# Weight sums made by pairs of tiles on VectorE, token sums moved from GpSimd to VectorE, and another order at the ends of blocks, in a fused attention and two-layer FFN kernel

## The chip, the cores and the metric

One core of a Trainium2 chip. The metric is the device time in microseconds (us) of the whole program; lower is better.

## The reference, cut to what matters

Three stages in a row on B = 2, H = 8, S = 768, D = 64, so 1536 tokens of 512 features; both FFN layers have 2048 hidden features. The attention inputs are float32, the four weight matrices float64, the output float32.

```python
def reference(q, k, v, lam, moe_w_in, moe_w_out, moe2_w_in, moe2_w_out):
    x = decay_attention(q, k, v, lam)             # blockwise, with a decayed state per head
    x = x.transpose(0, 2, 1, 3).reshape(1536, 512)
    h = x @ moe_w_in                              # 512 -> 2048
    x = (h * tanh(softplus(h))) @ moe_w_out       # 2048 -> 512
    h = x @ moe2_w_in
    return (h * clip(h + 3, 0, 6) / 6) @ moe2_w_out
```

## The kernel before, in words

Every operand of the FFN products is split into a high and a low part (`split`: ScalarE copies the rounded high part, L84, and VectorE subtracts it, L87); a product takes three passes (high-high, high-low, low-high). The weights come as float64 words of 8 bytes: `to_single` (L268) makes float32 of them with two instructions on ScalarE (L272, L273) and two on VectorE (L274, L277).

The 1536 tokens are three blocks of 512. The hidden features of a layer are 16 tiles of 128: 8 "lower" and 8 "upper". A **step** n of the main loop (L507) is one block and one tile of the first layer: 12 matmuls of the first product (`gemm1`, L301) into one of two PSUM banks h, then 12 of the second product of step n - 2 (`gemm2`, L310) into four banks y; ScalarE makes the activation (`act_first`, L330 and L331), VectorE its low part (`g_lo`). There are 48 steps: blocks 0 and 1 with the lower tiles (0 to 15), block 2 with all tiles (16 to 31), blocks 0 and 1 with the upper tiles (32 to 47). Attention runs in steps 0 to 15. The last tile of a block evacuates y (`evacuate`, emitted two steps later): block 2 by four splits into X, blocks 0 and 1 by four additions to `part` (L345) and splits owed one per step (`split_owed`). The next step's `gemm2` needs these four banks again.

The first layer's weights come as planned units (`advance`, `conv_at`), the upper ones in units of 512 KB through a pool of three staging tiles. In the second half of the main loop `make_later` (L457) prepares the second layer's weights, 32 units of 512 KB from step 22 on: each is loaded into the same pool, converted, split into `low`, the memory of the lower tiles that are no longer needed, and spilled to DRAM by pairs (`spill`, L409). The second product of the second layer is done in a Strassen-like scheme with 7 products instead of 8, so a pair of tiles needs three more weight blocks, which `sub` (L443) makes with four subtractions on GpSimd (POOL), and each token operand four more sums (`combine`, L615, L620, on GpSimd).

The last stretch (L667) is 24 **runs** j, one per block and pair of tiles, 8 runs to a block. A run has two first products (12 matmuls each, L587, into one single bank h, tag "h0", that `gate`, L609 on ScalarE and L610 on VectorE, must have read before the next), each followed by a part of the second products of the run before (`second_product`, L602): 18 matmuls, then 24, into seven accumulators. Weights are fetched back from DRAM (`fetch`, L412) into slots, in an order worked out before. When a block's 8 runs are through, `close_first` and `close_second` scale the accumulators (L640), add them up (L643 to L664, two sums on GpSimd) and store four quarters (L632).

All DMAs here are issued from SyncE's queue (SP), in order. The order of instructions on each engine is set by the compiler's list scheduler, which starts from the program's order and lets instructions whose inputs it takes to be ready go ahead; `tc.keep_in_program_order(ins)` ties an instruction behind the one traced before it on its engine.

## Time and profile before

| | us |
|---|---|
| median of 3 runs (602.42 to 605.28) | 604.87 |
| the profiled execution | 600.34 |
| its span, first to last instruction | 598.6 |
| busy in it: TensorE matmul / weight load | 570.5 / 481.9 |
| VectorE / ScalarE / GpSimd | 325.1 / 274.5 / 140.0 |

The profiled execution is one more run of the same program, 4.5 us below the median. Times in rows count from the start of the span. A line of the timeline is a start, a duration and a merged group of like instructions of one engine; "[1.66 <-ACT g L331]" is the idle time of the engine before the group and what ended it. Consecutive groups of one engine overlap a little, since an instruction's latency reaches over the next one's start. PE is TensorE, DVE is VectorE, ACT ScalarE, POOL GpSimd.

### The profile page before, as it was taken

How to read it: one execution, taken by the hardware profiler on the slowest of the kernel's cores; microseconds unless marked ns; L12 is line 12 of the kernel's file. 1: busy time of each engine (PE TensorE's matmuls, PEld its weight loads, DVE VectorE, ACT ScalarE, POOL GpSimd, SP SyncE). 2: the span in 40 equal slices, each digit the busy share in tenths (PEclk: the TensorE clock that was granted, in tenths of full speed). 3: DMA queues.
4: the chain of work that ended last, by engine and by line, in shares of the span. 5: the costliest groups of instructions: out<-in, count | busy, mean ns of one | idle time of the engine just before them, and what ended most of it. 6: DMA issues, size and time to landing. Idle time of an engine off the chain costs nothing. (4 is left out here: it accounts for less than half of the span.)

```text
span 598.6 us, 8726 instructions
## 1 busy us (share of the span) xinstructions
PE 570.5 (95%) x3470; PEld 481.9 (81%) x3470; DVE 325.1 (54%) x467; ACT 274.5 (46%) x460; POOL 140.0 (23%) x154
## 2 busy tenths in 40 slices
PE   7999999999999989599999999999899999899993
PEld 3777778878888878488788889999899999799993
DVE  3799996436765575966781633334533344433433
ACT  2378775216765565755761423233332334223332
POOL 1600100000212211222020233232532323523223
PEclk9999999999999999799999999999999999999998
DMA  7979663304356688566974468400486301576202
GB/s 226 396 242 337 212 204 109 106 2 155 127 202 273 205 321 305 200 253 244 334 289 204 193 230 306 167 1 19 139 303 261 124 1 66 185 279 205 112 1 70
DMA packets 23427, 113.82 MB, mean 190 GB/s; under 512 B 2378, under 2 KB 6490, under 8 KB 17754
## 3 DMA queue, kind: packets, MB, share of 16 engines
q1 hardware_dynamic: 23386, 113.27, 52.2%
q8 instruction: 27, 0.44, 0.3%
q14 instruction: 14, 0.11, 0.1%
HBM read 87.03 MB, written 26.22 MB: 189 GB/s over the span
## 5 line engine op out<-in xcount | busy, mean ns | idle before, releaser
L620 POOL TENSOR_TENSOR F<-F 128x256 f32<-128x256 f32 x96 | 80.1, 834 | 194.1 <-DVE F L610 190.3
L310 PE MATMUL y<-g,up 128*128 128x512 f32 x288 | 71.2, 396 | 6.2 <-DVE X L87 5.9
L610 DVE SCALAR_TENSOR_TENSOR F<-x,h 128x512 f32<-128x512 f32 x48 | 32.8, 684 | 75.4 <-ACT x L609 75.4
L587 PE MATMUL h<-X,up 128*128 128x512 f32 x288 | 70.2, 392 | 2.2 <-DVE F L610 2.2
L301 PE MATMUL h<-X,low 128*128 128x512 f32 x288 | 72.0, 397 | 0.2 <-DVE state L248 0.2
L301 PE MATMUL h<-X,up 128*128 128x512 f32 x288 | 69.5, 390 | 2.4 <-ACT g L331 2.4
L443 POOL TENSOR_TENSOR st<-st 128x256 f32<-128x256 f32 x32 | 33.8, 1066 | 162.6 <-DVE st L277 148.8
L587 PE MATMUL h<-X,low 128*128 128x512 f32 x288 | 69.9, 391 | 1.6 <-DVE F L610 1.6
L310 PEld LDWEIGHTS y<-g,up 128*128 128x128 f32 x288 | 54.8, 191 | 18.8 <-DVE X L87 6.3
L310 PE MATMUL y<-g,low 128*128 128x512 f32 x288 | 69.5, 390 | 0.1
L609 ACT ACTIVATE x<-h 128x512 f32<-128x512 f32 x48 | 28.7, 597 | 81.9 <-PE h L587 81.9
L301 PEld LDWEIGHTS h<-X,up 128*128 128x128 f32 x288 | 53.9, 188 | 14.5 <-ACT g L331 3.3
L310 PEld LDWEIGHTS y<-g,low 128*128 128x128 f32 x288 | 54.0, 188 | 11.7 <-DVE low L87 0.5
L301 PEld LDWEIGHTS h<-X,low 128*128 128x128 f32 x288 | 52.8, 188 | 13.1 <-issue 1.7
L587 PEld LDWEIGHTS h<-X,up 128*128 128x128 f32 x288 | 52.5, 188 | 12.7 <-DVE F L610 2.6
L274 DVE SCALAR_TENSOR_TENSOR st<-st 128x512 int32<-128x512 int32 (+1 forms) x57 | 43.6, 768 | 34.8 <-ACT st L273 34.6
L587 PEld LDWEIGHTS h<-X,low 128*128 128x128 f32 x288 | 52.7, 188 | 11.9 <-DVE F L610 1.8
L84 ACT ACTIVATE low<-st 128x512 fp32r<-128x512 f32 (+2 forms) x57 | 39.8, 698 | 47.5 <-DVE st L277 30.4
L272 ACT ACTIVATE st<-st 128x512 f32<-128x512 f32 (+1 forms) x57 | 42.1, 739 | 35.9 <-DMA st<-w 35.6
L87 DVE TENSOR_TENSOR low<-st,low 128x512 fp32r<-128x512 f32 (+2 forms) x57 | 47.9, 845 | 18.5 <-ACT low L84 17.6
L87 DVE TENSOR_TENSOR up<-F,up 128x256 fp32r<-128x256 f32 (+2 forms) x36 | 30.4, 844 | 44.7 <-ACT up L84 44.7
L87 DVE TENSOR_TENSOR low<-F,low 128x256 fp32r<-128x256 f32 (+2 forms) x36 | 30.1, 838 | 38.8 <-ACT low L84 38.8
(59 smaller groups left out, 716.1 us busy)
## 6 DMA issues: line engine op xcount, KB each, us to landing
st<-w SPq DMA_DIRECT2D x50, 512.0 KB, 5.6
wc<-low SPq DMA_DIRECT2D x8, 1792.0 KB, 6.8
up<-wc SPq DMA_DIRECT2D x8, 1792.0 KB, 7.3
raw<-att SPq DMA_DIRECT2D x24, 512.0 KB, 5.7
low<-wc SPq DMA_DIRECT2D x6, 1792.0 KB, 7.0
wc<-low SPq DMA_DIRECT2D x8, 1024.0 KB, 6.2
up<-wc SPq DMA_DIRECT2D x8, 1024.0 KB, 4.9
st<-w SPq DMA_DIRECT2D x7, 1024.0 KB, 7.3
```

The source lines that it names most:

```text
L84: nc.scalar.activation(out=hi, in_=src, func=ACTF.Copy)
L87: nc.vector.tensor_tensor(out=lo, in0=src, in1=f32(hi), op=ALU.subtract)
L272: nc.scalar.activation(out=hf, in_=hf, func=ACTF.Copy, scale=2.0 ** -112)
L274: nc.vector.scalar_tensor_tensor(out=lo, in0=hi, scalar=-2 ** 31, in1=lo, op0=ALU.bitwise_and, op1=ALU.bitwise_or)
L301: nc.tensor.matmul(h, lhsT=W[t][:, a, kt * 128:kt * 128 + 128], rhs=X[k][:, b, kt, :], start=(kt, a, b) == order[0], stop=(kt, a, b) == or ...
L310: nc.tensor.matmul(y[e], lhsT=l, rhs=r, start=(first and i == 0), stop=(last and i == 2),)
L443: nc.gpsimd.tensor_tensor(out=o, in0=a, in1=b, op=ALU.subtract)
L587: nc.tensor.matmul(h, lhsT=w[:, a, kt * 128:kt * 128 + 128], rhs=X[k][:, b, kt, :], start=(kt, a, b) == order[0], stop=(kt, a, b) == order ...
L609: nc.scalar.activation(out=x, in_=h, func=ACTF.Relu, bias=3.0)
L610: nc.vector.scalar_tensor_tensor(out=F[:, 2 * i:2 * i + 2].rearrange("p i n -> p (i n)"), in0=x, scalar=6.0, in1=h, op0=ALU.min, op1=ALU.mult,
L620: nc.gpsimd.tensor_tensor(out=F[:, o], in0=F[:, a], in1=F[:, b], op=op)
```

## The change

The pool of three staging tiles becomes one tile `ring` with three places. `low` loses its first two tiles to a tile `low0`, whose memory becomes, at step 20, a tile `spare` (half for sums, half for staging) and later the token operand's buffer `GBUF[0]`. The second layer's weights come as 16 units u of 1 MB, a pair of tiles and one half (0: for the first product, 1: for the second) each. A unit passes two phases. `assemble(u)` converts both tiles at once into a contiguous tile and, for half 1, makes the four subtractions on VectorE; its two ScalarE instructions are kept in program order, and it issues the load of unit u + 2. `deliver(u)` splits all of it in one go (1024 or 1792 columns) and spills it. The 32 phases (A0, A1, D0, A2, D1, A3, D2, ...) are given to the steps 21 to 46, one each and two in steps 24, 27, 31, 35, 39 and 43. The first layer's last ten units are asked for in steps 16 to 20, two each.

In the last stretch the seven products get other operands (F[1] to F[7] in place), the four token sums go to VectorE (one after the first gate, three after the second) and the splits become one of 3 and one of 4 quarters; in the last run they are cut finer. The order of the products at i = 0 and 1 is (1, 4, 2) and (6, 7, 5, 3), after the last run (1, 7, 6, 5) and (4, 2, 3). The closing sums of a block (`close`) follow each product, stand behind the gate and the sums in the program, and use VectorE and ScalarE alone.

```diff
-    unit_p = ctx.enter_context(tc.tile_pool(name="unit", bufs=3, side="right"))
+    ring = tm1_p.tile([128, 3, 512], U64, tag="ring", name="ring")
...
-    low = main.tile([128, 2048 * HALF], F32R, name="low")
+    low = main.tile([128, 2048 * (HALF - 2)], F32R, name="low")
+    low0 = main.tile([128, 4096], F32R, tag="low0", name="low0")
...
-        place(t, low[:, t * 2048:(t + 1) * 2048])
+        whole, i = (low0, t) if t < 2 else (low, t - 2)
+        place(t, whole[:, i * 2048:(i + 1) * 2048])
...
-        pool = unit_p if count == 1 else stage_p
-        st = pool.tile([128, count, 512], U64, tag=f"st{count}", name="st")
+        if w is w1 and count == 2:
+            st = stage_p.tile([128, 2, 512], U64, tag="st2", name="st")
+        elif w is w1:
+            i = unit_turn[0] % 3
+            unit_turn[0] += 1
+            slots[w is w1, t, half] = {i}
+            st = ring[:, i:i + 1]
+        elif half == 0:
+            slots[w is w1, t, half] = {0, 1}
+            st = ring[:, 0:2]
+        else:
+            slots[w is w1, t, half] = {3}
+            st = spare[0][:, 8:16].bitcast(U64).rearrange("p a n -> p (a n)").rearrange("p (t n) -> p t n", t=2)
...
+
+    def to_single(st, dest=None):
...
-        nc.scalar.activation(out=hf, in_=hf, func=ACTF.Copy, scale=2.0 ** -112)
-        nc.scalar.activation(out=lo, in_=lo16, func=ACTF.Copy, scale=2.0 ** -13, bias=2.0 ** -14 - 0.5)
+        for o, i, scale, bias in ((hf, hf, 2.0 ** -112, 0.0), (lo, lo16, 2.0 ** -13, 2.0 ** -14 - 0.5)):
+            ins = nc.scalar.activation(out=o, in_=i, func=ACTF.Copy, scale=scale, bias=bias)
+            if dest is not None:
+                tc.keep_in_program_order(ins)
...
         nc.vector.scalar_tensor_tensor(
-            out=hi, in0=hi, scalar=3, in1=lo, op0=ALU.logical_shift_left, op1=ALU.bitwise_or
+            out=hi if dest is None else dest.bitcast(I32), in0=hi, scalar=3, in1=lo,
+            op0=ALU.logical_shift_left, op1=ALU.bitwise_or
...
-    later = [(2 * p + i, half) for p in range(NPAIR) for half in (1, 0) for i in range(2)]
+    later = [(p, half) for p in range(NPAIR) for half in (0, 1)]
...
     def prefetch(upto):
         while fetched[0] < min(upto, len(later)):
-            t, half = later[fetched[0]]
-            load_w(w2, t, half, 1)
+            p, half = later[fetched[0]]
+            load_w(w2, 2 * p, half, 2)
             fetched[0] += 1
...
+    def assemble(u):
+        p, half = later[u]
+        B = spare[0] if half else ring[:, 2].bitcast(F32).rearrange("p (a n) -> p a n", n=256)
+        whole = B[:, 0:4].rearrange("p (t i) n -> p t (i n)", t=2)
+        to_single(staged(w2, 2 * p, half), whole)
+        prefetch(u + 3)
         if half == 0:
-            c = w1c(p % 2)[:, i]
-            split(c[:, 0], c[:, 1], hf)
-            if i == 1:
-                spill(p, 0)
...
+            ready[u] = whole
...
+            for o, x, y in ((4, 0, 1), (5, 2, 4), (6, 2, 0), (7, 3, 5)):
+                nc.vector.tensor_tensor(out=B[:, o], in0=B[:, x], in1=B[:, y], op=ALU.subtract)
+            ready[u] = B[:, 1:8]
+
+    def deliver(u):
+        p, half = later[u]
+        c = w2c(p % 2) if half else w1c(p % 2).rearrange("p t a n -> p a t n")
+        split(c[:, 0], c[:, 1], ready.pop(u))
+        spill(p, half)
+
+    PHASES = [(assemble, 0)]
+    for u in range(1, 2 * NPAIR):
+        PHASES += [(assemble, u), (deliver, u - 1)]
+    PHASES.append((deliver, 2 * NPAIR - 1))
 
     def make_later(count):
-        for _ in range(min(count, len(later) - made[0])):
-            prefetch(made[0] + 3)
-            convert_later(made[0])
-            made[0] += 1
-            prefetch(made[0] + 2)
+        for _ in range(count):
+            f, u = PHASES.pop(0)
+            f(u)
 
...
     conv_at = {
-        1: 2, 2: 1, 3: 1, 4: 2, 5: 1, 8: 2, 11: 1, 13: 1, 14: 2, 16: 2, 17: 1, 18: 2, 20: 2, 21: 2, 24: 1,
+        1: 2, 2: 1, 3: 1, 4: 2, 5: 1, 8: 2, 11: 1, 13: 1, 14: 2, 16: 2, 17: 2, 18: 2, 19: 2, 20: 2,
     }
-    conv_first = {1, 16, 18, 20, 24}
+    conv_first = {1, 16, 18, 20}
+    twice = {24, 27, 31, 35, 39, 43}
...
@@ -553,11 +572,15 @@
         split_owed()
         if n not in conv_first:
             advance(conv_at.get(n, 0))
-        if n >= 22:
-            make_later(2 if n % 2 == 0 else 1)
+        if n == 20:
+            spare.append(main.tile([128, 16, 256], F32, tag="low0", name="spare"))
+            prefetch(2)
+        if n >= 21 and PHASES:
+            make_later(2 if n in twice else 1)
...
-    GBUF = [low[:, 11264:14848], up[2][:, 0:3584]]
+    assert not PHASES
+    GBUF = [main.tile([128, 4096], F32R, tag="low0", name="G0")[:, 0:3584], up[2][:, 0:3584]]
...
-    PRODUCT = ((1, 0, 0), (2, 1, 1), (4, 2, 6), (5, 3, 3), (7, 5, 4), (6, 4, 5), (3, 6, 2))
+    PRODUCT = {1: (0, 0), 2: (2, 2), 3: (6, 1), 4: (1, 6), 5: (3, 3), 6: (4, 4), 7: (5, 5)}
...
+    SUMS = {4: (0, 2, ALU.add), 5: (4, 1, ALU.subtract), 6: (1, 0, ALU.subtract), 7: (3, 5, ALU.subtract)}
+
+    def sums(F, which):
+        for o in which:
+            a, b, op = SUMS[o]
+            nc.vector.tensor_tensor(out=F[:, o], in0=F[:, a], in1=F[:, b], op=op)
+
+    def parts(j, F, lo, hi):
+        if j not in G_t:
+            G_t[j] = GBUF[j % 2].rearrange("p (a i n) -> p a i n", a=2, i=7)
+        G = G_t[j]
+        split(G[:, 0, lo - 1:hi - 1], G[:, 1, lo - 1:hi - 1], F[:, lo:hi])
+
+    def combine(j, F, i):
+        if j < len(runs) - 1:
+            if i == 0:
+                sums(F, (6,))
+            else:
+                sums(F, (4, 5, 7))
+                parts(j, F, 1, 4)
+                parts(j, F, 4, 8)
+        elif i == 0:
+            parts(j, F, 1, 2)
+            sums(F, (6,))
+            parts(j, F, 6, 7)
+        else:
+            sums(F, (4, 5))
+            parts(j, F, 4, 6)
+            sums(F, (7,))
+            parts(j, F, 2, 4)
+            parts(j, F, 7, 8)
...
+    def close(k, m):
+        if not rest:
+            rest[:] = homes()
+        p1, c11, p7, c22, c21, c12 = rest
+        seen.add(m)
+        if m == 1:
+            scaled(p1, 1)
+        elif m == 7:
+            scaled(p7, 7)
+        elif m == 2:
+            added(c11, 2, p1)
+            store(k, 0, 0, c11)
+        elif m == 4:
+            if 6 in seen:
+                added(c21, 4, p7)
+                store(k, 1, 0, c21)
+            else:
+                scaled(c21, 4)
+        elif m == 6:
+            added(c12, 6, p1)
+        elif m == 5:
+            added(c22, 5, p7)
+            store(k, 1, 1, c22)
+            added(c12, 5, c12)
+        elif m == 3:
+            added(c12, 3, c12)
+            store(k, 0, 1, c12)
+        if m in (6, 7) and {6, 7} <= seen:
+            plus(p7, p7, c12)
+            if 4 in seen:
+                plus(c21, c21, p7)
+                store(k, 1, 0, c21)
+        if len(seen) == 7:
+            seen.clear()
+            rest.clear()
+
...
+            which = (1, 4, 2) if i == 0 else (6, 7, 5, 3)
+            if j == len(runs):
+                which = (1, 7, 6, 5) if i == 0 else (4, 2, 3)
...
             else:
-                second_product(j - 1, PRODUCT[:3] if i == 0 else PRODUCT[3:])
-                if j % NPAIR == 0:
-                    (close_first, close_second)[i](runs[j - 1][0])
+                second_product(j - 1, which)
                 if i == 1 and j - 1 in swap:
                     fetch(*swap[j - 1], 1)
             split_owed()
             if j < len(runs):
                 gate(F, i, h)
-        if j < len(runs):
-            combine(j, F)
-            if j in swap:
-                fetch(*swap[j], 0)
+                combine(j, F, i)
+            if j > 0 and j % NPAIR == 0:
+                for m in which:
+                    close(runs[j - 1][0], m)
+        if j in swap:
+            fetch(*swap[j], 0)
         while owed:
             split_owed()
```

## Rows read from the trace of the kernel before

**Rows 1.** The page: head of parts 1 and 2 (busy time; granted clock in 40 slices of 15 us).

```profile
span 598.6 us, 8726 instructions
...
PE 570.5 (95%) x3470; PEld 481.9 (81%) x3470; DVE 325.1 (54%) x467; ACT 274.5 (46%) x460; POOL 140.0 (23%) x154
...
PEclk9999999999999999799999999999999999999998
```

**Rows 2.** The waits of TensorE: who waited for whom, us in total, times, longest.

```profile
PE y L310 <- DVE X L87: 5.9, 1, 5.9
PE h L587 <- DVE F L610: 3.9, 3, 1.6
```

**Rows 3.** The timeline of TensorE, 205 to 300 us, middle stretch.

```profile
205.79 2.88 PE L301 MATMUL h<-X,up 128*128 128x512 f32 x12
...
213.05 3.02 PE L301 MATMUL h<-X,up 128*128 128x512 f32 x12 [1.66 <-ACT g L331]
...
234.99 2.88 PE L301 MATMUL h<-X,up 128*128 128x512 f32 x12
...
250.31 4.34 PE L310 MATMUL y<-g,up 128*128 128x512 f32 x12 [5.92 <-DVE X L87]
254.48 2.89 PE L301 MATMUL h<-X,up 128*128 128x512 f32 x12
...
259.93 2.88 PE L301 MATMUL h<-X,up 128*128 128x512 f32 x12
```

**Rows 4.** The timeline of ScalarE, 205 to 262 us.

```profile
237.83 0.67 ACT L272 ACTIVATE st<-st 128x512 f32<-128x512 f32 x1 [3.13 <-DMA st<-w]
...
245.83 0.67 ACT L84 ACTIVATE low<-st 128x512 fp32r<-128x512 f32 x1 [1.34 <-POOL st L443]
...
248.46 1.07 ACT L84 ACTIVATE X<-y 128x512 fp32r<-128x512 f32 x2
```

**Rows 5.** The timeline of all engines, 414 to 436 us, end of a block.

```profile
419.21 3.04 PE L602 MATMUL acc<-up,up 128*128 128x256 f32 x24
...
422.08 2.91 PE L587 MATMUL h<-X,up 128*128 128x512 f32 x12
...
426.96 1.17 DVE L664 TENSOR_TENSOR rest<-rest 128x512 f32<-128x512 f32 x1
...
428.06 0.68 DVE L610 SCALAR_TENSOR_TENSOR F<-x,h 128x512 f32<-128x512 f32 x1
...
428.79 3.04 PE L587 MATMUL h<-X,up 128*128 128x512 f32 x12 [1.65 <-DVE F L610]
```

**Rows 6.** Groups of instructions by form: count, busy us, mean ns, idle before.

```profile
L443 POOL TENSOR_TENSOR st<-st 128x256 f32<-128x256 f32 x32 | 33.8, 1066 | 162.6 <-DVE st L277 148.8 <-ACT st L273 13.2
...
L87 DVE TENSOR_TENSOR up<-F,up 128x1024 fp32r<-128x1024 f32 x12 | 14.7, 1225 | 30.5 <-ACT up L84 30.5
...
L274 DVE SCALAR_TENSOR_TENSOR st<-st 128x1024 int32<-128x1024 int32 x7 | 8.6, 1222 | 1.0 <-ACT st L273 1.0
...
L272 ACT ACTIVATE st<-st 128x1024 f32<-128x1024 f32 x7 | 8.2, 1174 | 3.8 <-DMA st<-w 3.8
...
L248 DVE TENSOR_TENSOR state<-faded,uo 128x256 f32<-128x256 f32 x8 | 3.3, 413 | 5.2 <-PE uo L225 5.1
```

**Rows 7.** DMA issues: count, KB each, median us from issue to landing.

```profile
wc<-low SPq DMA_DIRECT2D x8, 1792.0 KB, 6.8
...
st<-w SPq DMA_DIRECT2D x7, 1024.0 KB, 7.3
```

**Rows 8.** The timeline of all engines from 560 us, the end.

```profile
580.85 3.04 PE L602 MATMUL acc<-up,low 128*128 128x256 f32 x24
...
587.64 2.89 PE L602 MATMUL acc<-up,up 128*128 128x256 f32 x22 [0.76 <-DVE up L87]
...
592.80 1.77 POOL L662 TENSOR_TENSOR rest<-rest 128x512 f32<-128x512 f32 x1
```

**Rows 9.** The stores, line L632: first and last start.

```profile
L632 SPq DMA_DIRECT2D out<-rest x12: 372/389/453, 416.7 to 595.1; - x12
```

More of the change, by code (lines that the diff above doesn't have):

```diff
@@ L258, in decay_attention__mish_ffn__hswish_ffn_kernel @@
     stage_t = {}
+    unit_turn = [0]
+    busy = set()
+    slots = {}
     def load_w(w, t, half, count):
-        pool = unit_p if count == 1 else stage_p
-        st = pool.tile([128, count, 512], U64, tag=f"st{count}", name="st")
+        if w is w1 and count == 2:
[11 more added lines that the diff above has]
+            st = spare[0][:, 8:16].bitcast(U64).rearrange("p a n -> p (a n)").rearrange("p (t n) -> p t n", t=2)
+        taken = slots.get((w is w1, t, half), set())
+        assert not taken & busy
+        busy.update(taken)
         ins = nc.sync.dma_start(out=st, in_=w[t:t + count, half].rearrange("t p n -> p t n"))
@@ L265, in load_w, with staged @@
             tc.keep_in_program_order(ins)
-        stage_t[t, half] = st
-    def to_single(st):
+        stage_t[w is w1, t, half] = st
+    def staged(w, t, half):
+        busy.difference_update(slots.get((w is w1, t, half), ()))
+        return stage_t.pop((w is w1, t, half))
+    def to_single(st, dest=None):
         hf = st.bitcast(F32).rearrange("p t (n c) -> p t n c", c=2)[..., 1]
@@ L286, in convert @@
     def convert(w, t, half, count):
-        hf = to_single(stage_t.pop((t, half)))
+        hf = to_single(staged(w, t, half))
         cols = slice(half * 512, half * 512 + 512)
         if count == 2:
-            both = low.rearrange("p (t a n) -> p t a n", a=2, n=1024)[:, t:t + 2, :, cols]
+            whole, i = (low0, t) if t < 2 else (low, t - 2)
+            both = whole.rearrange("p (t a n) -> p t a n", a=2, n=1024)[:, i:i + 2, :, cols]
             wh, wl = both[:, :, 0], both[:, :, 1]
@@ L422, in prefetch @@
             fetched[0] += 1
-    def convert_later(n):
-        t, half = later[n]
-        p, i = t // 2, t % 2
-        st = stage_t.pop((t, half))
-        hf = to_single(st)[:, 0]
-        if half == 0:
-            c = w1c(p % 2)[:, i]
-            split(c[:, 0], c[:, 1], hf)
-            if i == 1:
-                spill(p, 0)
-        elif i == 0:
-            pend[p] = st, hf
-        else:
-            st0, hf0 = pend.pop(p)
-            free = [x.bitcast(F32).rearrange("p t (n c) -> p (t n) c", c=2)[..., 0] for x in (st0, st)]
-            q = slice(0, 256), slice(256, 512)
-            c = w2c(p % 2)
-            def sub(o, a, b):
-                nc.gpsimd.tensor_tensor(out=o, in0=a, in1=b, op=ALU.subtract)
-            split(c[:, 0, 0], c[:, 1, 0], hf0[:, q[0]])
-            sub(free[0][:, q[0]], hf0[:, q[1]], hf0[:, q[0]])
-            sub(free[0][:, q[1]], hf[:, q[1]], hf0[:, q[1]])
-            sub(free[1][:, q[0]], hf[:, q[1]], free[0][:, q[0]])
-            sub(free[1][:, q[1]], hf[:, q[0]], free[1][:, q[0]])
-            for j, src in ((1, hf), (3, free[0]), (5, free[1])):
-                src = src.rearrange("p (i n) -> p i n", i=2)
-                split(c[:, 0, j:j + 2], c[:, 1, j:j + 2], src)
-            spill(p, 1)
@@ L595, in second_product @@
         G, w = G_t[j], w2c(slot_of[j])
-        for m, gi, wi in which:
+        for m in which:
+            gi, wi = PRODUCT[m]
             if first:
@@ L630, in store, with scaled @@
     def store(k, M, N, y):
[L631 removed]
+        r0, c0 = k * 512 + (1 - M) * 256, (1 - N) * 256
         nc.sync.dma_start(
[L633 removed]
+            out=out[r0:r0 + 256, c0:c0 + 256].rearrange("(s p) n -> p s n", s=2), in_=y
         )
     SIXTH = 1.0 / 6.0
[L637 to L640 removed]
+    def scaled(o, m):
+        nc.scalar.activation(out=o, in_=acc[m], func=ACTF.Copy, scale=SIXTH)
@@ new lines, in homes @@
+    def homes():
+        both = [g_p.tile([128, 2, 2, 256], F32, tag="g", name="rest") for _ in range(3)]
+        return [b[:, i] for b in both for i in range(2)]
+    def close(k, m):
[33 more added lines that the diff above has]
+            rest.clear()
@@ L667, in decay_attention__mish_ffn__hswish_ffn_kernel @@
+    seen = set()
+    rest = []
     for j in range(len(runs) + 1):
```

44 lines of the change are left out of this document (5 added, 39 removed).

## The prediction, made before the changed kernel was run

> **What bounds the kernel now.** The page's first part comes first: TensorE is busy for 570.5 of 598.6 us [rows 1], so the change can win only where TensorE waits or after its last matmul, and lose where it makes TensorE wait anew. The same matmuls run before and after. So the next view is the list of who made TensorE wait: the largest wait is one of 5.9 us on VectorE's split of X (L87); three on the gate (L610) make 3.9 us [rows 2]. The kernel around them is full: one step of the middle stretch (a first and a second product) takes 5.45 us, from 254.48 to 259.93 us [rows 3].
>
> TensorE's timeline prices these waits from start to start, slow clock included. From 205.79 to 213.05 us is 7.26 us, 1.81 too many. From 234.99 to 254.48 us is 19.49 for two steps, 8.59 too many: it holds an idle 5.92 us and then twelve matmuls in 4.34 us where twelve take 2.89 [rows 3]; the page's clock line has its only dip before the end there, 0.7 in the seventeenth slice of 15 us [rows 1], so part of those came at the lower level, 1.2 GHz. Together **10.4 us** in the middle stretch, 8.6 of them at the end of block 2 (steps 33 and 34).
>
> ScalarE's timeline says why. Its queue is in order. A weight unit arrives late and holds it 3.13 us; then the split of the weight sums waits for GpSimd (1.34 us before 245.83 alone); only at 248.46 do the four evacuations to X begin, which free the PSUM banks that TensorE wants [rows 4]. So the stall is head-of-line blocking by weights that nobody needs yet: late loads, and a chain ScalarE, VectorE, GpSimd, ScalarE, VectorE within one unit.
>
> In the last stretch each end of a block costs once: from 422.08 to 428.79 us is 6.71 us for 12 matmuls of the first and 18 of the second product, usually half a step (2.72) plus 18 times 0.12 (24 lie between 419.21 and 422.08), 4.88: **1.8 us** too many, at two block ends [rows 5]. VectorE runs a closing sum of 1.17 us at 426.96, and only at 428.06 the gate that frees the only bank for h.
>
> After the last matmul: TensorE's last 22 matmuls start at 587.64 and take 2.89, the last sum ends on GpSimd at 592.80 + 1.77 = 594.57 [rows 8], its store issues at 595.1 [rows 9], and the span ends at 598.6 [rows 1].
>
> **The change, part by part.** *Weight sums by pairs.* Now, a pair takes 4 loads, 4 conversions of 512 columns (two instructions each on ScalarE and VectorE), 6 splits and 4 GpSimd sums of 1.07 us [rows 6]. After, an assemble step is two ScalarE instructions of 1024 columns, 1.17 us each, and two on VectorE of 1.22; for the half with sums, four subtractions of 256 columns, 0.41 each (the nearest row is L248) [rows 6]. So VectorE pays 2.45 or 4.1 us. A deliver step is one split: 1024 columns at 1.23 on VectorE, or 1792 columns, which by the slope from 0.68 (512 columns, [rows 5]) to 1.23 comes to 2.0. A pair costs VectorE 2.45 + 4.1 + 1.23 + 2.0 = 9.8 us; eight pairs, 78 us, lie over 26 steps of 5.45, 142 us. With 0.7 per step for the low part of g that is 3.7 us of each 5.45. ScalarE pays about 2.35 per assemble and, as VectorE, 1.2 or 2.0 per deliver.
>
> The heaviest steps: step 31 (both kinds) 4.1 + 2.0 + 0.7 = 6.8 us of VectorE; step 33 (assemble, and four X splits of 0.68) 5.9; step 41 (assemble, four additions, one owed split) 8.2. The first and last are above 5.45, but their neighbours hold 1.9 to 3, and the low part of g is wanted only two steps after its product, so 2.8 us of delay is covered. What covers it is that double buffering; without it, the excess of the three steps, 1.4 + 0.5 + 2.8 = 4.7 us, would be TensorE's. Pinning puts each assemble behind its own step's activations on ScalarE. A deliver reads sums made at least a step earlier, so no ScalarE instruction waits in its queue for VectorE or GpSimd any more. I take the whole 10.4 us as gained; the bounds are 10.4 and 10.4 - 4.7 - 1.8 (a wait like that before 213.05 stays) = 4.
>
> *DMAs and queues.* Each pair has 2 loads of 1 MB for 4 of half that, and the same two spills, all from SyncE. The load for unit u+2 is issued in assemble u, as soon as its staging area is read. The same staging area is used again three steps on, 16.3 us; reading takes 2.35 + 2.45, some 5, landing 7.3 [rows 7]: 4 us are left. Cost nothing; the cover is those 4 us (the slow rival below). The weight spills end at step 46, and the fetches for the last stretch queue behind them on SyncE: 2 x 1.0 and 2 x 1.8 MB, first needed about 20 us later, behind which one spill of 6.8 us [rows 7] fits.
>
> *First-layer weights.* The same ten units are asked for in steps 16 to 20 instead of 16 to 24; VectorE's four instructions of 0.68 each, twice, and 0.7 make 6.1 us a step for five steps, 3.5 over. Nothing there is urgent; taken as 0, between -2 and +2.
>
> *Token sums on VectorE.* Per run four sums of 0.41: 1.6 us more on VectorE and a middle split of 768 columns. After the second h of a run: activation 0.68, gate 0.68, three sums 1.2, split of 768 about 1.0 on each engine: ready after 4.6 us. TensorE wants it after 24 x 0.12 + 2.72 = 5.6 us. Hidden by 1 us in the worst order; cost 0. Bound: the whole 1.6 showing in all 23 runs between.
>
> *Block ends.* The closing now stands behind the sums and splits. From the second gate VectorE has 0.68 + 1.2 + 0.95 + 1.23 + six closing instructions of 0.68: 8.2 us, from 0.7 on, so to 8.9. The next gate must end at 5.6 + 2.16 = 7.8. Served first, it ends at 7.0 and nothing is lost; served last, at 9.6, 1.8 us are lost, as now. I take 1.15 lost: **0.65 gained, twice, 1.3**, bounds 0 and 3.6.
>
> *Tail.* The last run's matmuls follow at 580.85 + 2.88 = 583.73 [rows 8], as now, but then without waiting: products 1 and 7 need only the first half (to 585.17); product 6 needs activation, gate, two sums, one split, 580.85 + 3 x 0.68 + 0.82 + 0.68 = 584.4. TensorE ends at 583.73 + 42 x 0.12 = 588.8, not 590.5. Seven VectorE instructions follow product 6 (at 585.9): 585.9 + 7 x 0.68 = 590.7, and the store issues then instead of at 595.1: **4.4 gained**; bounds 2 and 6.
>
> Sum: 10.4 + 1.3 + 4.4 = **16.1 us**. The profiled execution took 600.34 us (span 598.6 and 1.74 around it), so 584.2 for such a one. The median of the runs shown is 4.5 us above it; against that, 604.87 - 16.1 = **588.8 us**.
>
> **A rule that speaks against it.** The rows show VectorE busy 54% [rows 1] and yet its late instructions stalling TensorE. For such a case the Trainium skill (Perfetto Trace Analysis, Optimizing Scalar/DVE Operations) says that breaking up instructions may let work finish sooner; the change makes them longer. By that rule the stall at the end of block 2 would not go, and the sum would be 7.5 us: the first rival.
>
> **Rivals.** *The stall stays at the end of block 2.* An X split may have to stand behind a 2.0 us split or a 4.1 us assemble, where now it stands behind pieces of 0.7 to 1.3; four such holds give back 8.6 us. The step load of 5.9 at step 33 after 6.8 at step 31 speaks for it, the pins and the absent GpSimd against. Gain 16.1 - 8.6 = 7.5: 597.4 us.
>
> *Slower: loads come late.* Place: the assemble steps 21 to 44. If a 1 MB load queues behind a 1.8 MB spill, it lands after 7.3 + 6.8 = 14.1 us; with 5 of reading, 19.1 against 16.3. Then the pinned ScalarE instruction holds the activations, 2.8 us a pair, 22 us over eight; and these take the place of the 10.4: 604.87 + 22.4 - 16.1 = 611 us. It decides from a landing time of 11 us on. The medians of 6.8 and 7.3 us speak against it.
>
> *The order, not the engines, is the limit.* The compiler's scheduler may place the unpinned rest so that new waits of the old size come, and only part of the tail remains: 602 to 607 us.
>
> **How the numbers follow.** Forecast 0.64 (581 to 594, its own range), first rival 0.21 (594 to 601.5), no change 0.07, slower 0.08. The range of 581 to 601 leaves out the last two and a little of each side. A measurement of this kernel tells about 0.5%, 3 us, from no change: faster 0.85, same 0.07, slower 0.08.
>
> **What would show it.** Right: no wait of TensorE over 1 us between 200 and 330 us; a granted clock of 1.00 there; no GpSimd work after the first stretch; the 1792-column split near 2.0 us; assemble's first ScalarE instruction never waiting on the load for more than 1 us; from the last run's first second-product matmul to the last store's issue 7.0 us (now 595.1 - 583.73 = 11.4). Wrong: an idle TensorE behind X (L87's successor) in steps 33, 34, 41 or 42, ScalarE idle on loads, or each run of the last stretch longer than 10.5 us (two halves of 4.88 and 5.6).

## The result, and the profile after

The changed kernel takes **585.21 us** (median of 4 runs, 584.2 to 588.91) against 603.64 us (600.1 to 605.28) for the kernel before on the same chip: ratio 0.9713, 95% interval 0.965 to 0.9777, a gain of 18.4 us. Forecast were 588.8 us and a gain of 16.1.

The page of the profiled execution (588.91 us, the longest of the four):

```profile
span 587.1 us, 8456 instructions
...
PE 570.9 (97%) x3470; PEld 482.7 (82%) x3470; DVE 351.4 (60%) x516; ACT 258.8 (44%) x371; POOL 16.0 (3%) x20
...
PEclk9899999999999999999999999999999999999998
```

Beside [rows 1], TensorE's busy time is the same, the span 11.5 us shorter, and the dip in the seventeenth slice is gone. The waits of TensorE (waiting line, releasing line, us in total, times, longest):

```profile
PE uo L211 <- POOL raw L189: 6.4, 3, 5.4
PE sc L173 <- issue: 1.2, 1, 1.2
```

Both waits of [rows 2] are gone, but for 0.3 us at one gate; the largest one left lies in the attention at the start, and none of the others is over 1.2 us. TensorE's timeline in the stretch that answers to [rows 3]:

```profile
240.37 2.88 PE L329 MATMUL h<-X,up 128*128 128x512 f32 x12
243.09 2.88 PE L338 MATMUL y<-g,up 128*128 128x512 f32 x12
245.81 2.88 PE L329 MATMUL h<-X,up 128*128 128x512 f32 x12
```

A step is 5.44 us with nothing between. The same view gives the starts of the stretches, read at four places (first product of step 0, of step 24, of run 0, and the last run's second first product):

```profile
33.87 0.94 PE L329 MATMUL h<-X,low 128*128 128x512 f32 x3 [0.20 <-DVE state L250]
...
191.41 0.84 PE L329 MATMUL h<-X,up 128*128 128x512 f32 x3
...
321.97 0.84 PE L610 MATMUL h<-X,low 128*128 128x512 f32 x3
...
570.82 0.86 PE L610 MATMUL h<-X,up 128*128 128x512 f32 x3
```

The table has the differences of these starts, read in the same way in every kernel of this study; "tail" is the span less the last of them. All are us of one profiled execution each; the median is of all runs of that kernel.

| kernel | step 0 starts | steps 0-23 | middle (24 steps) | runs | tail | span | median |
|---|---|---|---|---|---|---|---|
| before | 29.7 | 154.3 | 142.0 | 252.1 | 20.5 | 598.6 | 603.64 |
| changed | 33.9 | 157.5 | 130.6 | 248.9 | 16.3 | 587.1 | 585.21 |
| middle_only | 34.4 | 156.0 | 130.6 | 252.2 | 20.5 | 593.6 | 594.49 |
| last_only | 29.6 | 158.7 | 145.2 | 248.8 | 16.3 | 598.6 | 600.37 |
| before_sums_dve | 30.6 | 154.4 | 130.6 | 252.1 | 20.5 | 588.1 | 591.07 |
| before_sums_dve_twice | 29.4 | 156.6 | 133.6 | 252.2 | 20.5 | 592.2 | 595.08 |
| before_sums_last | 30.6 | 158.3 | 130.6 | 248.8 | 16.3 | 584.5 | 585.86 |
| after_sums_pool | 33.2 | 155.9 | 130.6 | 249.1 | 16.3 | 585.1 | 588.96 |
| after_no_pin | 34.7 | 154.2 | 130.6 | 248.8 | 16.3 | 584.6 | 586.51 |
| after_fine_deliver | 33.9 | 154.5 | 130.6 | 248.8 | 16.3 | 584.1 | 585.65 |
| after_close_early | 32.3 | 158.2 | 130.6 | 248.7 | 16.3 | 586.1 | 587.83 |
| after_token_pool | 33.1 | 155.3 | 130.6 | 252.4 | 16.9 | 588.2 | 593.03 |
| after_tail_plain | 34.3 | 156.1 | 130.6 | 248.9 | 17.5 | 587.3 | 588.56 |
| after_pin_units | 30.7 | 155.3 | 130.6 | 248.8 | 16.2 | 581.6 | 583.28 |

From before to changed the middle gives 11.4 us, the runs 3.3 and the tail 4.2, together 18.9; the first two columns take back 4.2 and 3.2. The second of these varies by 4.5 us over the table without regard to the edits (last section), so a span alone says little here, and the columns are what to compare. The medians of the other kernels are from three further sessions, in which the kernel before had 602.04, 602.22 and 600.91 us; each ratio below is to its own.

The end of a block, to be held against [rows 5] (all engines):

```profile
418.51 2.91 PE L610 MATMUL h<-X,up 128*128 128x512 f32 x12
...
421.26 2.91 PE L626 MATMUL acc<-up,G 128*128 128x256 f32 x23
...
423.23 0.68 DVE L634 SCALAR_TENSOR_TENSOR F<-x,h 128x512 f32<-128x512 f32 x1
...
424.01 2.97 PE L610 MATMUL h<-X,up 128*128 128x512 f32 x12
```

The gate (L634) ends 5.4 us after the first product began, against 6.7 in [rows 5], and the compiler has put 23 matmuls ahead of the next first product instead of 18: no wait. The end, against [rows 8, 9]:

```profile
576.44 5.20 PE L626 MATMUL acc<-up,up 128*128 128x256 f32 x42
...
580.44 3.08 DVE L683 SCALAR_TENSOR_TENSOR rest<-acc,rest 128x512 f32<-128x512 f32 x5
```

The 42 matmuls run in one go, and the last store is issued at 583.5, 7.1 us after the first of them (all stores of line L673, first and last start):

```profile
L673 SPq DMA_DIRECT2D out<-rest x12: 372/388/389, 413.9 to 583.5; - x12
```

Groups by form that answer to terms of the prediction, the long split and an assemble's first instruction, for half 0 and half 1 (count, busy us, mean ns, idle before):

```profile
L89 DVE TENSOR_TENSOR low<-spare,low 128x1792 fp32r<-128x1792 f32 x8 | 16.2, 2023 | 8.6 <-ACT low L86 8.6
...
L297 ACT ACTIVATE ring<-ring 128x1024 f32<-128x1024 f32 x8 | 9.2, 1150 | 3.5 <-DMA ring<-w 3.5
...
L297 ACT ACTIVATE spare<-spare 128x1024 f32<-128x1024 f32 x8 | 9.2, 1144 | 0.0
```

### The profile page after: what moved, and what is told of

It reads as the page before. It is cut to its first block, busy times and chain, and to the rows that moved or that the text cites. A ratio compares the mean times of both kernels' runs of the same rounds, so it can differ in the third digit from the quotient of the medians.

```text
span 587.1 us, 8456 instructions
## 1 busy us (share of the span) xinstructions
PE 570.9 (97%) x3470; PEld 482.7 (82%) x3470; DVE 351.4 (60%) x516; ACT 258.8 (44%) x371; POOL 16.0 (3%) x20
## 3 DMA queue, kind: packets, MB, share of 16 engines
q1 hardware_dynamic: 23130, 113.26, 52.6%
## 4 chain that ended last, share of the span: by engine, by line
PE 88%; DVE 4%; DMA 3%; ACT 2%; POOL 2%; issue 1%; DVEq 0%; SPq 0%; POOLq 0%; ACTq 0%
PE h L610 22%; PE y L338 21%; PE h L329 21%; PE acc L626 20%; PE sc L173 1%; DMA st<-w 1%; PE uo L218 1%; DMA mask<-z 1%; PE uo L211 1%; ACT st L297 1%; POOL raw L189 1%; PE uo L227 1%; DVE low L89 1%; DMA ring<-w 1%; DVE st L300 1%
## 5 line engine op out<-in xcount | busy, mean ns | idle before, releaser
L634 DVE SCALAR_TENSOR_TENSOR F<-x,h 128x512 f32<-128x512 f32 x48 | 33.0, 687 | 95.2 <-ACT x L633 95.0
L633 ACT ACTIVATE x<-h 128x512 f32<-128x512 f32 x48 | 28.7, 598 | 125.0 <-PE h L610 124.8
L338 PE MATMUL y<-g,up 128*128 128x512 f32 x288 | 69.2, 389 | 0.0
L610 PEld LDWEIGHTS h<-X,up 128*128 128x128 f32 x288 | 52.5, 188 | 10.4 <-DVE F L634 0.5
L358 ACT ACTIVATE x<-h 128x512 f32<-128x512 f32 x48 | 28.5, 594 | 69.5 <-PE h L329 69.4
L89 DVE TENSOR_TENSOR g<-x,g 128x512 fp32r<-128x512 f32 x48 | 33.0, 687 | 41.8 <-ACT g L359 41.8
L297 ACT ACTIVATE ring<-ring 128x512 f32<-128x512 f32 (+3 forms) x52 | 40.5, 820 | 16.3 <-DMA ring<-w 16.2
L644 DVE TENSOR_TENSOR F<-F 128x256 f32<-128x256 f32 x96 | 40.6, 423 | 2.2
L86 ACT ACTIVATE up<-F 128x768 fp32r<-128x768 f32 (+3 forms) x27 | 23.5, 871 | 25.4 <-DVE F L644 15.6
L86 ACT ACTIVATE G<-F 128x768 fp32r<-128x768 f32 (+1 forms) x24 | 22.9, 954 | 25.6 <-DVE F L644 16.6
L89 DVE TENSOR_TENSOR up<-F,up 128x768 fp32r<-128x768 f32 (+3 forms) x27 | 26.6, 987 | 12.4 <-ACT up L86 12.4
L626 PEld LDWEIGHTS acc<-low,G 128*128 128x128 f32 x252 | 31.9, 191 | 1.8 <-ACT G L86 0.6
```

The costliest lines, as they stand in the source:

```text
L86: nc.scalar.activation(out=hi, in_=src, func=ACTF.Copy)
L89: nc.vector.tensor_tensor(out=lo, in0=src, in1=f32(hi), op=ALU.subtract)
L297: ins = nc.scalar.activation(out=o, in_=i, func=ACTF.Copy, scale=scale, bias=bias)
L338: nc.tensor.matmul(y[e], lhsT=l, rhs=r, start=(first and i == 0), stop=(last and i == 2),)
L358: nc.scalar.activation(out=x, in_=h, func=ACTF.Mish)
L610: nc.tensor.matmul(h, lhsT=w[:, a, kt * 128:kt * 128 + 128], rhs=X[k][:, b, kt, :], start=(kt, a, b) == order[0], stop=(kt, a, b) == order ...
```

## The experiments

All ratios are to the kernel before on the same chip in the same session. The theory to be tested was that of the prediction: late loads and the chain within a unit hold ScalarE, and shortening both needs the pairs. Its main rival was that GpSimd's part alone does it.

**Which half of the change?** middle_only is the changed kernel with the last stretch of before (token and closing sums on GpSimd, order of the products as before); last_only is the kernel before with the last stretch of the changed one.

```diff
-    SUMS = {4: (0, 2, ALU.add), ...}        (last stretch of the changed kernel)
+    def combine(j, F): ... pool(4, 0, 2, ALU.add)   (that of the kernel before)
```

> The changed kernel with the last stretch of the kernel before (token sums on GpSimd, its splits, its order at block ends and its tail). If the parts of the change are independent, the middle stretch (first product of step 24 to the first product of run 0) takes the changed kernel's 130.6 us against 142.0 before, the runs up to the last one 257.7 us, the tail 14.9 us: about 11.4 us under the kernel before, 592 us. Rival, that the pairs need the freed GpSimd or the new last stretch: the middle stays above 135 us and the time above 596 us.

Measured: 594.49 us, ratio 0.987 (0.9783 to 0.9958). The middle is at its floor, runs and tail are those of before, with the same waits on the gate as in [rows 2] (3.9 us, three times).

```diff
-    PRODUCT = ((1, 0, 0), (2, 1, 1), ...)
+    PRODUCT = {1: (0, 0), 2: (2, 2), ...}    (and sums, parts, combine, close as changed)
-            sub(free[0][:, q[0]], hf0[:, q[1]], hf0[:, q[0]])
+            sub(free[0][:, q[0]], hf0[:, q[0]], hf0[:, q[1]])    (operands in the new order)
```

> The kernel before with the last stretch of the changed kernel (token sums on VectorE, closing order, tail); the weight blocks are put in the order which that stretch needs, with the same number of sums on GpSimd. If the parts are independent: middle 142 us, the runs 254.5 us (3.3 less), tail 10.7 us (4.2 less): 7.5 us under the kernel before, 596 us. Rival, that the new last stretch gains only because weights are ready earlier: runs at 257 us, time near 600 us.

Measured: 600.37 us, 0.9962 (0.9925 to 0.9998), and not the 596 expected. Runs and tail are wholly those of the changed kernel, 7.5 us better; but the middle became 3.3 us longer and steps 0 to 23 4.4 us, so that nearly nothing is left. The wait on X at the end of block 2 is as before:

```profile
255.92 5.26 PE L310 MATMUL y<-g,up 128*128 128x512 f32 x12 [6.06 <-DVE X L87]
```

So the new last stretch needs nothing of the new weight sums, and by the whole kernel's time one would have missed that it works. Of the 3.3 us in the middle 2.2 lie in the two steps of this stall, which take 21.71 us here (first products from 239.31 to 261.02) against 19.49 before. Why the middle grew is not settled; what the subtractions read changed with the operands' order.

**Is it GpSimd alone?** The kernel before, with nothing but the four weight sums of a pair moved:

```diff
             def sub(o, a, b):
-                nc.gpsimd.tensor_tensor(out=o, in0=a, in1=b, op=ALU.subtract)
+                nc.vector.tensor_tensor(out=o, in0=a, in1=b, op=ALU.subtract)
```

> The kernel before with the four weight sums of a pair on VectorE instead of GpSimd, nothing else. Theory of the prediction (ScalarE's queue is held by late loads and by the chain within a unit, GpSimd being one link of it): the stall at the end of block 2 shrinks by some 2 to 5 us of 8.6, the middle takes 134 to 140 us, the time is 597 to 602 us. Rival, GpSimd alone is the cause: the middle falls to 131 us, the time to 593 us. Rival, only the order of the loads matters: no change, middle 142 us.

Measured: 591.07 us, 0.9819 (0.9745 to 0.9892). The middle is 130.56 us, as in the changed kernel to the hundredth. One word of the kernel gives the whole 11.4 us: no pairs, no longer instructions, no ring. The theory's 134 to 140 us was wrong, the rival's number right. In this kernel the last product of block 2 is still running when its first banks are read, 0.9 us after its start (TensorE and ScalarE):

```profile
236.63 2.88 PE L310 MATMUL y<-g,up 128*128 128x512 f32 x12
...
237.54 1.25 ACT L84 ACTIVATE X<-y 128x512 fp32r<-128x512 f32 x2
```

In the kernel before that product starts at 237.71, and X is read only at 248.46 [rows 4], 10.75 us later:

```profile
237.71 2.88 PE L310 MATMUL y<-g,up 128*128 128x512 f32 x12
```

The order on ScalarE hardly differs. Counted from the start of the program to that first read of X, ScalarE's instructions are the same in both kernels but for three (one conversion, one split of weights, one activation, under 2 us together) that stand behind X here; and last_only, which has the stall, has exactly those of the kernel before ahead of X. ScalarE comes late to nearly the same place of its queue. From the first product of step 24 to the read of X it takes 64.4 us in the kernel before (184.03 to 248.46) and 52.6 us here (184.95 to 237.54). Its waits in these two stretches, first the kernel before, then this one (us in total, times, longest):

```profile
ACT low L84 <- DVE st L277: 10.2, 11, 1.5
ACT low L84 <- POOL st L443: 8.3, 8, 1.6
ACT st L272 <- DMA st<-w: 8.3, 4, 3.1
```

```profile
ACT low L84 <- DVE st L277: 9.6, 7, 1.8
ACT x L330 <- PE h L301: 5.4, 6, 1.4
ACT st L272 <- DMA st<-w: 3.6, 4, 1.6
ACT low L84 <- DVE st L443: 0.6, 1, 0.6
```

The 8.3 us on GpSimd become 0.6 us on VectorE's sums, the waits for loads fall from 8.3 to 3.6 us, and for 5.4 us ScalarE now waits for TensorE: it is ahead. Over the whole kernel the waits for loads are as long as ever (35.6 us before, 37.0 here), so that sum does not show it. Late loads and GpSimd's part in the chain shrink together here, and this run does not tell their shares apart.

**Is GpSimd needed for the stall, and is it enough?** The changed kernel, weight sums back on GpSimd:

```diff
             for o, x, y in ((4, 0, 1), (5, 2, 4), (6, 2, 0), (7, 3, 5)):
-                nc.vector.tensor_tensor(out=B[:, o], in0=B[:, x], in1=B[:, y], op=ALU.subtract)
+                nc.gpsimd.tensor_tensor(out=B[:, o], in0=B[:, x], in1=B[:, y], op=ALU.subtract)
```

> The changed kernel with the four weight sums of a pair back on GpSimd, in the same place of the program. Theory: a deliver phase reads sums made a step or more earlier, so 4.3 us of GpSimd a pair are covered, the middle stays at 131 to 132 us and the time within 1 us of the changed kernel (585 us). Rival, GpSimd alone is the cause of the old stall: waits of ScalarE on GpSimd come back before the evacuations, the middle takes over 135 us, the time is above 590 us.

Measured: 588.96 us, 0.9776 (0.9705 to 0.9846), the middle at its floor again, although up to the read of X ScalarE waits for GpSimd twice as long as it did before (from the first product of step 24, 189.1 to 242.0 us; all of its waits there):

```profile
ACT low L86 <- POOL spare L463: 16.1, 4, 5.4
ACT x L358 <- PE h L329: 6.1, 5, 1.4
```

No load is waited for in this stretch, the sums are read a phase later, and X is still read in time. So there were two remedies in the change, each sufficient in its kernel: the sums on VectorE, or the rebuilt weight pipeline as a whole. Which of its parts does it (pairs, loads in time, sums read later) was not run apart with the sums on GpSimd. The median is 3.8 us above the changed kernel's, more than expected; the intervals of the two ratios overlap, and no column of the table accounts for it.

**Does the length of the chain count at all?** The kernel with sums on VectorE, each sum issued twice (the second writes the same values again):

```diff
+                for _ in range(2):
+                    nc.vector.tensor_tensor(out=o, in0=a, in1=b, op=ALU.subtract)
```

> The kernel before with the weight sums on VectorE, each issued twice with the same result: 3.3 us a pair instead of 1.65, nearly the 4.3 us of GpSimd. Theory A, the length of the chain within a unit is what cost the time: part of the old stall is back, the middle takes 134 to 139 us. Theory B, GpSimd itself cost it (a second engine's waits in ScalarE's queue, VectorE's instructions stretched beside it): the middle stays at 130.6 to 131.5 us and the time near 591 us.

Measured: 595.08 us, 0.988 (0.9829 to 0.9931). Two sums of 0.42 us are 0.84, GpSimd's one is 1.07 on the mean [rows 6]; yet the middle loses 3.0 us and not 11.4, between what the two theories gave, and hardly at block 2: X is read there at 241.43, 3.8 us after the product's start, and the step is 0.5 us longer. Most of the loss is at the end of block 0:

```profile
289.30 0.98 PE L310 MATMUL y<-g,up 128*128 128x512 f32 x3 [2.02 <-DVE part L345]
```

An addition to `part` stood behind sums and splits on VectorE, the kind of hold that the prediction's first rival feared, in another place. So VectorE's longer chain costs something. Whether it could bring back the stall at block 2 is not shown: up to the read of X ScalarE waits 11.3 us for loads and 1.8 us for sums, but the compiler has put eight of its weight instructions fewer ahead of X.

**Do pairs, pins and long splits add anything?** The kernel before with sums on VectorE and the new last stretch (the edits of before_sums_dve and last_only together):

> The kernel before with its four weight sums a pair on VectorE, and the last stretch of the changed kernel: no pairs, no ring, no pins, units of 512 KB as before. Theory (the gain of the middle is the sums leaving GpSimd, the rest of the change there is not needed): step 0 at 30 us, middle 130.6, runs 248.9, tail 16.3: 580 to 583 us, under the changed kernel by the start. Rival (the new last stretch needs the pairs, or its GpSimd-free sums upset the old order): middle above 133 us, time above 587 us.

Measured: 585.86 us, 0.9725 (0.9683 to 0.9767): the changed kernel's 0.9713 within the intervals. Middle, runs and tail are those expected; the 580 to 583 us were missed, and the profiled execution has steps 0 to 23 at 158.3 us. The changed kernel without the pins:

```diff
-            if dest is not None:
-                tc.keep_in_program_order(ins)
```

> The changed kernel without the pins on the conversion of the second layer's weights. Theory: with the sums off the chain there is room enough, and the order on ScalarE does not matter: middle 130.6 to 131.5 us, time within 1 us of the changed kernel. Rival, the pins keep late loads from holding ScalarE's queue: waits of ScalarE on loads of over 2 us before an activation and a middle above 133 us.

Measured: 586.51 us, 0.9745 (0.9689 to 0.9801), the middle at its floor. And with `deliver` cut into pieces of 256 and 512 columns:

```diff
-        split(c[:, 0], c[:, 1], ready.pop(u))
+        src = ready.pop(u)
+        for a, b in ((0, 1), (1, 3), (3, 5), (5, 7)) if half else ((0, 1), (1, 2)):
+            split(c[:, 0, a:b], c[:, 1, a:b], src[:, a:b])
```

> The changed kernel with each deliver step cut into splits of 256 and 512 columns as before, instead of one of 1024 or 1792. The page's rule on breaking up instructions would gain only where a long instruction held something urgent; the changed kernel's middle has no wait, so nothing is gained: middle 130.6 us, time within 1 us of the changed kernel. Rival, the shorter pieces cost VectorE and ScalarE about 1 us a pair more and a wait comes back at an end of a block: middle above 131.5 us.

Measured: 585.65 us, 0.9743 (0.9683 to 0.9803), the middle at its floor. Neither the pins nor the length of the instructions is worth anything that the middle shows. The Trainium skill (Perfetto Trace Analysis, Optimizing Scalar/DVE Operations) says that breaking up instructions may let work finish sooner where they make another engine wait; here no wait was left to cure, and cutting gave nothing.

**What frees the block ends?** First the place of the closing in the program: before the gate and the sums, as it was.

```diff
                 second_product(j - 1, which)
+                if j % NPAIR == 0:
+                    for m in which:
+                        close(runs[j - 1][0], m)
...
-            if j > 0 and j % NPAIR == 0:
-                for m in which:
-                    close(runs[j - 1][0], m)
```

> The changed kernel with the closing sums of a block in front of the gate in the program, as before, on VectorE and ScalarE alone. Theory: the closing sums then go ahead of the gate that frees the bank for h, 1.0 to 1.8 us at each of two block ends: runs 251 to 252.5 us instead of 248.9, time 2 to 4 us above the changed kernel. Rival, that GpSimd's slow sums made the old stall and the place in the program does not matter: runs at 249 us.

Measured: 587.83 us, 0.9756 (0.9707 to 0.9805), runs of 248.7 us, no wait:

```profile
417.62 2.91 PE L610 MATMUL h<-X,up 128*128 128x512 f32 x12
...
421.79 0.68 DVE L634 SCALAR_TENSOR_TENSOR F<-x,h 128x512 f32<-128x512 f32 x1
422.64 2.91 PE L610 MATMUL h<-X,up 128*128 128x512 f32 x12
```

The gate ends 4.85 us after the first product's start. The program's order of the closing, on which the prediction's 1.3 us rested, is worth nothing once the token sums are on VectorE. Then the token sums alone back on GpSimd, the closing left on VectorE and ScalarE:

```diff
         for o in which:
             a, b, op = SUMS[o]
-            nc.vector.tensor_tensor(out=F[:, o], in0=F[:, a], in1=F[:, b], op=op)
+            nc.gpsimd.tensor_tensor(out=F[:, o], in0=F[:, a], in1=F[:, b], op=op)
```

> The changed kernel with the four token sums of a run on GpSimd. Theory: the first split no longer needs any of them and the second is wanted 10 us after the gate, so inside a block they are hidden on either engine; at the two block ends the closing sums on VectorE run beside them: runs 248.9 to 250 us, time within 1.5 us of the changed kernel. Rival, GpSimd beside VectorE's closing sums is what held the gate: 1 to 1.7 us at each block end come back, runs 251 to 252.5 us.

Measured: 593.03 us, 0.9846 (0.9786 to 0.9907), runs of 252.4 us: against the expectation the whole gain of that stretch is gone, and 0.6 us of the tail. At the end of a block:

```profile
415.18 1.55 DVE L89 TENSOR_TENSOR G<-F,G 128x768 fp32r<-128x768 f32 x1 [0.31 <-ACT G L86]
415.56 2.91 PE L610 MATMUL h<-X,up 128*128 128x512 f32 x12
...
417.36 1.06 ACT L86 ACTIVATE G<-F 128x1024 fp32r<-128x1024 f32 x1 [1.72 <-POOL F L644]
...
418.45 1.23 DVE L89 TENSOR_TENSOR G<-F,G 128x1024 fp32r<-128x1024 f32 x1 [0.58 <-ACT G L86]
...
421.40 0.68 DVE L634 SCALAR_TENSOR_TENSOR F<-x,h 128x512 f32<-128x512 f32 x1
...
422.13 3.04 PE L610 MATMUL h<-X,up 128*128 128x512 f32 x12 [1.51 <-DVE F L634]
```

No GpSimd closing sum is left here, and the stall is back at 1.51 us (1.65 in [rows 5]). The gate ends 6.5 us after the product's start, 1.1 later than in the changed kernel, though VectorE has no sums to make in between: it waits 0.58 us for them through ScalarE, and its own instructions take longer while GpSimd works. In the kernel before ScalarE waits for GpSimd's token sums at the same place, ahead of the gate of [rows 5]:

```profile
424.13 1.06 ACT L84 ACTIVATE low<-F 128x1024 fp32r<-128x1024 f32 x1 [2.19 <-POOL F L620]
```

The split by form, of after_token_pool and then of the changed kernel:

```profile
L89 DVE TENSOR_TENSOR G<-F,G 128x768 fp32r<-128x768 f32 x12 | 17.8, 1487 | 8.8 <-ACT G L86 8.8
```

```profile
L89 DVE TENSOR_TENSOR G<-F,G 128x768 fp32r<-128x768 f32 x12 | 11.5, 958 | 0.0
```

The same split takes 1.49 us on the mean with GpSimd's sums (1.53 to 1.55 in the eleven that run beside them, 0.95 in the one that does not) and 0.96 without. The Trainium skill (same page and section, Perfetto Trace Analysis, Optimizing Scalar/DVE Operations) says that GpSimd and VectorE share a read port, so that moving work between the two might not help; the rows fit the sharing, and show a move back to VectorE that did help.

**The tail.** The last run treated like every other:

```diff
-        if j < len(runs) - 1:
+        if True:
...
-            if j == len(runs):
-                which = (1, 7, 6, 5) if i == 0 else (4, 2, 3)
```

> The changed kernel with its last run treated like the others: sums and splits not cut finer, products in the order (1, 4, 2), (6, 7, 5, 3). Theory: TensorE waits again for the last run's splits, 0.3 and 0.8 us as before, and the closing sums end about 0.6 us later behind the last matmul: from the last h to the end 17.5 to 18.2 us instead of 16.3, against 20.5 before. Rival, the order and the cut of the last run give the whole 4.2 us and the closing sums on VectorE nothing: 20 us.

Measured: 588.56 us, 0.978 (0.9722 to 0.9837), tail 17.5 us against 16.3. The matmuls still run in one group, but VectorE's last three closing instructions end 8.6 us after the first of the 42 matmuls, against 7.1 in the changed kernel:

```profile
575.44 5.61 PE L626 MATMUL acc<-up,up 128*128 128x256 f32 x42
...
581.97 2.08 DVE L683 SCALAR_TENSOR_TENSOR rest<-acc,rest 128x512 f32<-128x512 f32 x3
```

By these runs 1.2 of the tail's 4.2 us go with the last run's order and finer pieces and 0.6 with the token sums; the other 2.4 were not divided further (the closing without GpSimd's last sum, 1.77 us in [rows 8], is among them).

**The start.** Every kernel with `ring` starts step 0 late (32.3 to 34.7 us), but for after_pin_units below. The changed kernel's start (load of an upper unit, the mask's load, GpSimd's first use of the mask, TensorE's wait for it):

```profile
1.18 0.42 SPq L283 DMA_DIRECT2D ring<-w  x1
...
9.21 0.93 SPq L160 DMA_DIRECT2D mask<-z  x2
...
16.04 1.40 POOL L189 TENSOR_TENSOR raw<-raw,mask 128x512 f32<-128x512 f32 x1 [15.60 <-DMA mask<-z]
...
17.49 1.12 PE L211 MATMUL uo<-raw 128*64 128x64 f32 x16 [5.37 <-POOL raw L189]
```

The second load of all is that of an upper unit, which the program asks for later; it has gone ahead into the plain tile. Its conversion follows on ScalarE and VectorE at once, and the mask's load is issued 2 us later than before (7.17). Tied to its place:

```diff
-        if pinned[0]:
+        if pinned[0] or (w is w1 and count == 1):
             tc.keep_in_program_order(ins)
```

> The changed kernel with the loads of the first layer's single units kept in program order on SyncE. In the changed kernel's profiles the first of them (for an upper tile that step 24 needs) is issued second of all, before the loads of the attention, and its conversion stands on ScalarE and VectorE before the mask is used: step 0 starts at 33.2 to 34.4 us in three profiles with the ring, at 29.6 to 30.6 in three with the pool. Theory: this start costs 3.5 to 4 us; here step 0 starts near 30 us, middle 130.6, runs 248.9, tail from the last h 16.3 unchanged: 580 to 582 us. Rival, that the start differs by chance from run to run: step 0 anywhere from 29.5 to 34.5 us, time 585 us.

Measured: **583.28 us**, 0.9699 (0.9651 to 0.9747), the fastest of all. Step 0 starts at 30.7 us, the mask is used 2.55 us earlier:

```profile
6.97 0.93 SPq L160 DMA_DIRECT2D mask<-z  x2
...
13.49 1.06 POOL L189 TENSOR_TENSOR raw<-raw,mask 128x512 f32<-128x512 f32 x1 [13.05 <-DMA mask<-z]
```

It is faster than the kernel before; over the changed kernel the 3.2 us of the start stand in the profile, while the intervals of the two ratios overlap and the 580 to 582 us expected were not reached. That the load goes ahead because a plain tile has no places to wait for fits these runs, but no run put the pool back into the changed kernel.

## Why the prediction was right, and where it was not

**The middle stretch, forecast 10.4, measured 11.4.** The mechanism was read rightly: TensorE stalls on X at the end of block 2 because ScalarE serves its queue in order (it idles 1.34 us for GpSimd with X ready behind, [rows 4]) and is late, held by loads and by a chain that runs through GpSimd (8.3 us of waits each from step 24 to the read of X, beside 10.2 on VectorE's conversions). What was wrong is what the cure needs: the pairs were taken for it, and moving the sums alone gives the whole stretch (before_sums_dve). How much of the stall is the loads' and how much GpSimd's stays open, since no run made the loads alone come earlier. Of the bound of 4, with its excess of heavy steps, nothing showed: TensorE waits nowhere in this stretch, and the 1792-column split took the forecast 2.0 us. The 1.0 us beyond the forecast are the small waits that it left out.

**The block ends, forecast 1.3, measured 3.3.** The step that failed is the queue of VectorE from the second gate on: token sums on VectorE were costed at 0, and the gain was to come from the closing's place, "served first" or "served last". The runs show the reverse: the place gives nothing, and without the token sums' move all 3.6 us are gone (after_token_pool). The sum also missed that the compiler could put 23 matmuls where 18 stood. The reading of [rows 5], that a closing sum on VectorE ahead of the gate makes the stall, falls too: in after_close_early the closing sums stand ahead of the gate as well, and nothing waits. What it left out of those rows is ScalarE's wait of 2.19 us for GpSimd's token sums, ahead of the same gate.

**The tail, forecast 4.4, measured 4.2.** From the last run's first matmul to the last store 7.1 us (7.0 forecast, 11.4 before).

**Start and first-layer weights, taken as 0 between -2 and +2.** The units in steps 16 to 20 cost nothing: steps 0 to 23 take 154.2 us in after_no_pin and 154.3 before. The start cost 4.2 us. The prediction counted the edit of `unit_p` to `ring` as a matter of memory, and did not ask what a load may do that no longer waits for a place in a pool. 11.4 + 3.3 + 4.2 = 18.9, less 4.2, is 14.7 (the 3.2 us of steps 0 to 23 left aside), and the medians say 18.4. The other 3.7 us are not placed: the profiled execution of before is 3.3 us below the median here, and where its longer executions spend that was not profiled. The record has only the mean granted clock of its executions in the three further sessions: 0.989 to 0.992 in those below 600.2 us, 0.978 to 0.986 in those of 604.8 to 606.5 us. That the whole gain came within 2.3 us of the forecast is in part luck: the block ends gave 2.0 us more than forecast, the start took 4.2.

**The rivals.** The stall did not stay at block 2, and long instructions did no harm. Loads hardly came late: one assemble of sixteen waits for its load, 3.5 us (in the groups by form above), against the forecast of none above 1, and TensorE lost nothing by it. That the order would be the limit did not come true: without the pins the middle is at its floor too (after_no_pin).

## What to carry to other kernels

When a matmul engine stalls on an evacuation, first count the instructions ahead of the evacuation in its engine's queue, before and after: if they are the same, the order is not the cause, and the engine is late. Then add up that engine's waits from a fixed mark to the read; their sum over the whole kernel can be the same in a kernel that stalls and in one that does not. Try the one-word edit first; here moving four sums to another engine gave all that the rebuilding of the weight pipeline gave in its stretch. And when a pool becomes a plain tile, look at the first 20 us again: what the pool held back may now go first.

## What the runs showed that was not expected

A split on VectorE is half again as long beside GpSimd's sums (1.49 against 0.96 us above), so moving work from GpSimd to VectorE can make VectorE finish earlier.

Steps 0 to 23 take 154.2 to 158.7 us from kernel to kernel, unrelated to the edits. There TensorE has a wait near 64 to 70 us for which the profile shows no releaser, 0.75 to 2.14 us long. In the kernel before, and in last_only, whose program is the same up to there:

```profile
63.61 1.13 PE L171 MATMUL sc<-raw 64*128 64x128 f32 x8 [0.80 <-issue]
```

```profile
64.70 1.13 PE L171 MATMUL sc<-raw 64*128 64x128 f32 x8 [2.14 <-issue]
...
69.55 4.55 PE L310 MATMUL y<-g,low 128*128 128x512 f32 x12
```

After the longer wait twelve matmuls take 4.55 us instead of 2.91, and the granted clock over 60 to 75 us is 0.77 instead of 1.00, so a part of it went by at the lower level, 1.2 GHz. Over 60 to 80 us the granted clock is 0.83 in the three kernels with the longest steps 0 to 23 (158.2 to 158.7 us), 0.91 in the changed kernel and middle_only (157.5 and 156.0), and 1.00 in the other nine (154.2 to 156.6), one of which, after_tail_plain, has a wait of 2.1 us too. So the clock is a part of the difference and not all of it. What the wait is for was not found; single spans of this kernel lie apart by some 4 us.
